# Attention and gated feed-forward in one kernel: fp32 weights by hardware DMA with casts on ACT and VectorE, and a first batch loaded in 1 KB rows

## The chip, the cores and the metric

The kernel runs on one core of one Trainium2 chip. The metric is the device time of one execution in microseconds (us). The chip's engines are called PE (TensorE), ACT (ScalarE), DVE (VectorE), POOL (GpSimd) and SP (SyncE). POOL and SP issue the DMAs here.

## The reference, cut to what matters

```python
# q, k, v: (8 batches, 8 heads, 576, 64) fp32; global_idx: 8 positions
scores = (q @ k^T) / 8, kept where |i - j| <= 32, or i or j is a global position
x = softmax(scores) @ v             # heads side by side: 4608 tokens x 512
g, val = x @ w_gate, x @ w_val      # 512 x 1536 each
ffn_out = (gelu(g) * val) @ w_out   # 1536 x 512
out = x + sigmoid(x @ w_res) * ffn_out   # 4608 x 512 fp32
```

All inputs are fp32. The kernel computes in bf16 with fp32 accumulation.

## The kernel before

The 4608 tokens are cut into nine *chunks* of 512. A *stage* is the feed-forward of one chunk: twelve blocks of up-projection (`ffn_in`, 8 matmuls each), then sixteen steps of down-projection (`ffn_out`). The attention of the next chunk is woven into the down-projection. Chunk c + 1 has tokens of batches c and c + 1, so the weave of stage c needs batch c + 1 to be loaded.

Everything that arrives as fp32 and is wanted as bf16 is loaded by POOL, whose DMA casts on the way. Only the first batch's Q and K come raw through SP. The parts that the change touches:

```python
def load_qk(b):                       # POOL, casting: 10 DMAs in 256 B rows
    for src, dst in ((q, q_st), (k, k_st)):
        for r in range(NQT):
            ...
            nc.gpsimd.dma_start(dst[0:n, r, :]..., src[b]...)

def load_v(b):                        # POOL, casting: 5 DMAs into ve[b % 2]
    ...
def shift_v(b):                       # SP: vo[b % 2] is ve moved by 64 partitions
    nc.sync.dma_start(vo[b % 2][0:64, ...], ve[b % 2][64:128, ...])
    nc.sync.dma_start(vo[b % 2][64:128, ...], ve[b % 2][0:64, ...])
def turn_qk(b):                       # SP: 10 DMA transposes, q_st -> qt, k_st -> kt
    ...
def zero_rest(i, eng):
    eng.memset(ve[i][:, :, :, D:VG], 1.0)      # V's column of ones: L161
    eng.memset(ve[i][0:32, 0, :, :], 0.0)
    ...                                        # five more small ones

# first batch: raw Q and K, a head pair at a time, on 96 partitions
for p in range(NP):
    for src, what in ((q, "q"), (k, "k")):
        nc.sync.dma_start(raw[what][0:QP, ...], src[0, 2 * p:2 * p + 2]...)
...
gather("k", 0); gather("q", 0); zero_rest(0, nc.gpsimd); load_v(0); gather("v", 0)
load_gate_cols(0, 512)
... # masks, transposes and scores of batch 0
load_gate_cols(512, 1024)
...
load_qk(1)
load_gate_cols(1024, 1536)
load_v(1)
nc.gpsimd.dma_start(wr_t, ...)
for h0 in range(0, NFF, 6):
    nc.gpsimd.dma_start(wo_t[:, h0:h0 + 6, :], ...)
for n in range(1, B // 2):            # nine gathers of the global rows
    for what in "kqv":
        gather(what, n)
...
for c in range(NCH):
    b = c + 1
    if b < B:
        if c == 0: zero_qk(1)
        turn_qk(b)
        if b > 1: load_v(b)
    for j in range(NFF):
        ffn_in(c, j)
        if b < B:
            if c == 0 and j == 1:
                zero_rest(1, nc.vector)        # after load_v(1) in program order
                hot_rows(1)
            ...
            if j == 8:
                shift_v(b)
                if b + 1 < B: load_qk(b + 1)
                prep_qz(b, 0, NP)
            if j == 11:
                held = global_scores(b)        # sg (needs qt), ss (needs kt)
    ... # scores, values, turn_x of chunk c + 1 woven into ffn_out(c)
```

`turn_x(c, t)` makes the transposed x of a chunk. For c > 0 the tiles 0 to 2 go through SP's DMA transpose and tile 3 through PE.

The softmax here doesn't subtract the row's maximum and nothing guards it: scores larger than these inputs give would overflow.

## Time and profile before

| | before |
|---|---|
| median of the runs | 433.5 us (432.92 to 435.04, 4 runs) |
| profiled span | 431.6 us |
| PE busy | 386.6 us, 90% of the span |
| mean granted PE clock | 0.974 |
| up-projection of chunk 0 | 34.3 to 77.5 us, 20.2 of it idle |
| first matmul of chunk 1's up-projection | 98.8 us |
| stage 1 | 42.9 us |

The two rows below are from the page's busy digits of the kernel before. Each digit is the busy share, in tenths, of one fortieth of the span (10.8 us).

```profile
PE   2578009999999999999999999999999999999995
DMA  7999998949997999399849992996296130021001
```

The zeros in the fifth and sixth place are the gap. The DMA row is full from the second to the sixth slice, so the gap falls where the DMA engines have no room. From the seventh slice on PE has no hole. The next view cuts the same stretch into pieces. Its columns are the window, its length, then the busy time and instruction count of PE, PEld, DVE, ACT and POOL, then the granted clock, a DMA share (not used here) and GB/s.

```profile
43.99:64.21 20.22, 0.00 (x1) 0.00 (x0) 1.92 (x7) 0.00 (x0) 8.04 (x10) 0.59 1.55 160
...
77.34:98.82 21.48, 21.32 (x210) 13.44 (x212) 11.11 (x23) 10.34 (x16) 10.59 (x12) 1.00 1.06 109
```

In the first row PE, PEld and ACT do nothing for 20.2 us while DMA goes on. In the last row, the down-projection of chunk 0 with the attention of chunk 1 in it, PE is busy for 21.3 of 21.5 us.

### The profile page before, as it was taken

How to read it: one execution, taken by the hardware profiler on the slowest of the kernel's cores; microseconds unless marked ns; L12 is line 12 of the kernel's file. 1: busy time of each engine (PE TensorE's matmuls, PEld its weight loads, DVE VectorE, ACT ScalarE, POOL GpSimd, SP SyncE). 2: the span in 40 equal slices, each digit the busy share in tenths (PEclk: the TensorE clock that was granted, in tenths of full speed). 3: DMA queues.
4: the chain of work that ended last, by engine and by line, in shares of the span. 5: the costliest groups of instructions: out<-in, count | busy, mean ns of one | idle time of the engine just before them, and what ended most of it. 6: DMA issues, size and time to landing. Idle time of an engine off the chain costs nothing.

```text
span 431.6 us, 7189 instructions
## 1 busy us (share of the span) xinstructions
PE 386.6 (90%) x2749; PEld 208.9 (48%) x2794; DVE 209.6 (49%) x396; ACT 169.6 (39%) x274; POOL 167.9 (39%) x194
## 2 busy tenths in 40 slices
PE   2578009999999999999999999999999999999995
PEld 1363004654465446544654565456545654564442
DVE  6774027554656355535544554356435644463421
ACT  5455002623462336333623462345235423533320
POOL 6577252915492471257125712561330120022012
PEclk9999758999999999999999999999999999999999
DMA  7999998949997999399849992996296130021001
GB/s 173 169 178 155 161 164 170 109 93 112 146 92 111 101 178 120 66 124 182 88 87 112 185 89 77 128 184 73 74 147 93 38 98 1 0 75 62 0 26 74
DMA packets 164642, 46.56 MB, mean 108 GB/s; under 512 B 152128, under 2 KB 158784, under 8 KB 164608
## 3 DMA queue, kind: packets, MB, share of 16 engines
q0 software_dynamic: 108784, 18.62, 60.5%
q1 hardware_dynamic: 55824, 27.48, 33.0%
q8 instruction: 22, 0.36, 0.4%
q14 instruction: 12, 0.10, 0.1%
HBM read 39.19 MB, written 9.44 MB: 113 GB/s over the span
## 4 chain that ended last, share of the span: by engine, by line
PE 74%; issue 8%; POOL 1%; DVE 1%; POOLq 0%; DVEq 0%
PE f_ps L432 19%; PE v_ps L409 18%; PE g_ps L405 17%; PE r_ps L422 6%; PE nd L373 4%; PE sc L347 3%; PE nd L367 2%; PE sn L335 2%; PE sg L313 2%; POOL ob L438 1%; PE ss L318 1%; DVE qz L306 1%; PE tx L397 0%; POOLq L570 0%; DVE ht L413 0%
## 5 line engine op out<-in xcount | busy, mean ns | idle before, releaser
L409 PE MATMUL v_ps<-xt,wv_t 128*128 128x512 bf16 x431 | 111.8, 382 | 21.0 <-DVE ht L413 20.4
L412 ACT ACTIVATE gsb<-g_ps 128x512 bf16<-128x512 f32 x108 | 64.5, 597 | 145.8 <-PE g_ps L405 112.4
L413 DVE SCALAR_TENSOR_TENSOR ht<-gsb,v_ps 128x512 bf16<-128x512 bf16 x108 | 73.9, 687 | 91.7 <-PE v_ps L409 90.1
L438 POOL TENSOR_TENSOR ob<-prb,xtok 128x512 f32<-128x512 f32 x36 | 41.9, 1164 | 193.3 <-DVE prb L436 193.2
L405 PE MATMUL g_ps<-xt,wg_t 128*128 128x512 bf16 x415 | 109.4, 381 | 1.1 <-ACT xt L398 0.7
L432 PE MATMUL f_ps<-wo_t,ht 128*128 128x512 bf16 x412 | 102.0, 380 | 1.0
L409 PEld LDWEIGHTS <-wv_t 128*128 128x128 bf16 x432 | 42.5, 98 | 72.5 <-issue 22.3
L405 PEld LDWEIGHTS <-wg_t 128*128 128x128 bf16 x432 | 42.4, 98 | 52.0 <-issue 1.9
L432 PEld LDWEIGHTS <-ht 128*128 128x128 bf16 x432 | 38.4, 98 | 34.0
L350 ACT ACTIVATE pt<-sc 128x512 bf16<-128x512 f32 x72 | 41.8, 597 | 29.1 <-PE sc L347 29.0
L425 ACT ACTIVATE rsb<-r_ps 128x512 bf16<-128x512 f32 x36 | 21.4, 596 | 62.0 <-PE r_ps L422 58.0
L352 DVE TENSOR_TENSOR pt<-pt,maskw 128x512 bf16<-128x512 bf16 x72 | 31.8, 444 | 26.7 <-ACT pt L350 25.6
L90 POOL DMA_DIRECT2D q_st<-in_q_dram x35 | 29.8, 868 | 24.0 <-DMA qt<-q_st 24.0
L436 DVE SCALAR_TENSOR_TENSOR prb<-rsb,f_ps 128x512 f32<-128x512 bf16 x36 | 24.6, 684 | 29.4 <-PE f_ps L432 29.2
L422 PE MATMUL r_ps<-wr_t,xt 128*128 128x512 bf16 x137 | 36.6, 379 | 0.4
L98 POOL DMA_DIRECT2D ve<-in_v_dram x40 | 34.3, 869 | 1.9 <-DMA k_st<-in_k_dram 1.9
L90 POOL DMA_DIRECT2D k_st<-in_k_dram x35 | 30.8, 908 | 2.8 <-issue 1.2
L347 PE MATMUL sc<-qz,kt 128*128 128x128 bf16 x288 | 27.8, 224 | 0.0
L347 PEld LDWEIGHTS <-kt 128*128 128x128 bf16 x288 | 21.7, 100 | 12.1
L387 DVE TENSOR_TENSOR xtok<-nd,rden 128x512 bf16<-128x512 f32 x34 | 23.5, 692 | 1.2
L373 PEld LDWEIGHTS <-pt 128*128 128x128 bf16 x576 | 22.3, 97 | 1.8 <-DMA vo<-ve 0.8
L373 PE MATMUL nd<-ve,pt 128*128 128x65 bf16 x320 | 22.4, 193 | 0.0
(104 smaller groups left out, 259.7 us busy)
## 6 DMA issues: line engine op xcount, KB each, us to landing
out_dram<-ob SPq DMA_DIRECT2D x36, 256.0 KB, 2.1
vo<-ve SPq DMA_DIRECT2D x16, 260.0 KB, 5.7
q_st<-in_q_dram POOLq DMA_DIRECT2D x28, 128.0 KB, 5.0
k_st<-in_k_dram POOLq DMA_DIRECT2D x28, 128.0 KB, 6.1
ve<-in_v_dram POOLq DMA_DIRECT2D x24, 128.0 KB, 6.7
ve<-in_v_dram POOLq DMA_DIRECT2D x16, 96.0 KB, 6.0
wg_t<-in_moe_w_gate_dram POOLq DMA_DIRECT2D x3, 512.0 KB, 5.9
wv_t<-in_moe_w_val_dram POOLq DMA_DIRECT2D x3, 512.0 KB, 12.7
```

Source lines behind the costliest of these rows:

```text
L90: nc.gpsimd.dma_start(dst[0:n, r, :].rearrange("p (h d) -> p h d", d=D), src[b].rearrange("h s d -> s h d")[128 * r:128 * r + n])
L98: nc.gpsimd.dma_start(t[p0:p1, c, :, 0:D], v[b].rearrange("h s d -> s h d")[s0 + p0:s0 + p1])
L347: nc.tensor.matmul(sc[:, n, :, :], kt[b % 2][:, p, 64 * i:64 * i + 128], qz[b % 2][:, p, :, 64 * i:64 * i + 64], start=True, stop=True)
L350: nc.scalar.activation(mine, sc, ACTF.Exp, bias=0.0, scale=SCALE)
L373: nc.tensor.matmul(nds[h // 4][:, VG * (h % 4):VG * (h % 4) + VG], view(pt, 0, 128, c0, [[1, 128]]), vw, start=False, stop=(h % 4 == 3 and ...
L405: nc.tensor.matmul(g_ps, wg_t[:, kk, 128 * j:128 * j + 128], x[:, kk, :], start=(kk == 0), stop=(kk == NKT - 1))
L409: nc.tensor.matmul(v_ps, wv_t[:, kk, 128 * j:128 * j + 128], x[:, kk, :], start=(kk == 0), stop=(kk == NKT - 1))
L412: nc.scalar.activation(gsb, g_ps, ACTF.Gelu, bias=0.0, scale=1.0)
L413: nc.vector.scalar_tensor_tensor(ht[:, j, :], gsb, 0.5, v_ps, ALU.mult, ALU.mult)
L422: nc.tensor.matmul(r_ps, xt[c % 2][:, kk, 128 * t:128 * t + 128], wr_t[:, kk, :], start=(kk == 0), stop=(kk == NKT - 1))
L432: nc.tensor.matmul(held["f"], ht[:, j, 128 * t:128 * t + 128], wo_t[:, j, :], start=(j == 0), stop=(j == NFF - 1))
L438: nc.gpsimd.tensor_tensor(ob, prb, xtok[c % 2][:, t, :], ALU.add)
```

## The change

The intent is to take the weights out of POOL's queue. Each weight is cut into fp32 pieces of 512 KB, loaded by SP's hardware DMA into tiles that are not needed until batch 1, and cast from there by DVE and ACT between the blocks of chunk 0. The first batch's raw Q and K come in 1 KB rows on all 128 partitions, and the scores run as each head pair arrives. Because the pieces occupy tiles of batch 1, that batch is loaded later than before.

```diff
+    slots = [flat32(qz[1], 0), flat32(qz[1], 1024), flat32(xt[1], 0), flat32(xtok[1], 0), flat32(vo_flat[1], 0),
+             flat32(kt[1], 0), flat32(qt[1], 0), flat32(ve_flat[1], 0)]
+    pieces = [...]          # 12 of w_gate and w_val, 2 of w_res, 6 of w_out
+    def load_piece(n):
+        nc.sync.dma_start(staged(n), pieces[n][0])
+    def cast_piece(n, copy):
+        copy(pieces[n][1], staged(n))
+        nxt = NSL + n if n < NRE else n + NRE if n >= NSL else len(pieces)
+        if nxt < len(pieces):
+            load_piece(nxt)
-    RPP = 6
+    RPP = 4
 ...
     for c in range(NCH):
         b = c + 1
         if b < B:
-            if c == 0:
-                zero_qk(1)
-            turn_qk(b)
-            if b > 1:
+            if c:
+                turn_qk(b)
                 load_v(b)
         for j in range(NFF):
             ffn_in(c, j)
             if b < B:
                 if c == 0:
+                    ... # cast_piece(4) to cast_piece(19), one or two a block
-                    if j == 1:
+                    if j == 6:
+                        zero(q_st[:, :, 0:1])
+                        zero(k_st[:, :, 0:1])
+                        load_qk(1)
+                    elif j == 9:
                         zero_rest(1, nc.vector)
+                        load_v(1)
                         hot_rows(1)
+                    elif j == 11:
+                        shift_v(1)
                 if c == 1:
+                    if j == 0:
+                        for n in range(1, B // 2):
+                            for what in "kqv":
+                                gather(what, n)
 ...
+        if c == 0:
+            jobs[0] += [lambda: zero_qk(1), lambda: turn_qk(1)]
+            jobs[4].append(ready)          # prep_qz(1, 0, NP); load_qk(2)
+            jobs[5].append(second)         # global_scores(1)
+            ...
+            for t in range(4):
+                jobs[(11, 12, 14, 15)[t]].append(lambda t=t: values(1, t))
+                jobs[(13, 14, 16, 16)[t]].append(lambda t=t: turn_x(1, t))
```

`jobs[n]` runs ahead of step n of the down-projection, and `jobs[16]` after the last step. Numbers of steps below are these.

## The prediction

> **What bounds the kernel now.** I read the page first: PE is busy 90% of the span, and from slice 8 on its digits are all 9, so the seven later stages are matmul time and nothing that the change does to them can give much. The room is in the first 80 us. There I read the timelines of PE, of VectorE (DVE), of GpSimd (POOL) and of the sync queue in turn. PE first (columns: start us, duration us, engine, line, operation, count, idle time before it):
>
> ```profile
> 42.97 1.03 PE L405 MATMUL g_ps<-xt,wg_t 128*128 128x512 bf16 x4
> 64.21 1.87 PE L409 MATMUL v_ps<-xt,wv_t 128*128 128x512 bf16 x4 [20.22 <-DVE ht L413]
> ...
> 77.34 1.14 PE L313 MATMUL sg<-qt,kgz 128*128 128x288 bf16 x8
> ```
>
> The up-projection of chunk 0 starts at 34.3, stops at 44.0 and resumes at 64.2. The first group after the gap takes 1.87 us where a warm one takes 1.03: a cold clock, worth some 2 us until 68.7. Without the gap, 12 column blocks at 2 x 0.864 us would take 20.7 us; they take 43. What held `ht` stands in DVE's timeline:
>
> ```profile
> 38.06 0.69 DVE L413 SCALAR_TENSOR_TENSOR ht<-gsb,v_ps 128x512 bf16<-128x512 bf16 x1 [1.05 <-PE v_ps L409]
> 61.88 0.09 DVE L161 MEMSET ve<- 128x40 bf16 x1 [23.14 <-DMA ve<-in_v_dram]
> ```
>
> The memset of V's ones column for batch 1 waits in program order for V of batch 1 to land, and that load sits in GpSimd's queue behind the weights. DVE stands still, and four to five blocks later so does PE. Behind that is a full DMA system: the DMA row of the page is at 9 until about 72 us. The gap is thus partly an order problem and partly a lack of DMA time. What batch 1 needs after its loads is in the sync queue, here for batch 2:
>
> ```profile
> 101.50 6.63 SPq L302 DMA_TRANSPOSE qt<-q_st  x5
> 108.24 6.45 SPq L302 DMA_TRANSPOSE kt<-k_st  x5
> ```
>
> Ten DMA transposes take 13.2 us of issue, and in the other stages it is 13.4 to 14.6. In GpSimd's timeline the loads that come before them take:
>
> ```profile
> 120.52 4.26 POOL L90 DMA_DIRECT2D q_st<-in_q_dram  x5
> 124.74 4.24 POOL L90 DMA_DIRECT2D k_st<-in_k_dram  x5
> ...
> 143.86 4.24 POOL L98 DMA_DIRECT2D ve<-in_v_dram  x5
> ```
>
> So Q, K and V of one batch are 8.5 + 4.2 us[...], and the page gives some 6 us (5.0 to 6.7) from issue to landing.
>
> [...]raw Q/K by hardware DMA, V by GpSimd and part of the first weights together fill the DMA row from 5 to 19 us.[...] Here the raw loads on 96 partitions ran at 240 to 250 GB/s, the 128-partition output stores at about 370.[...]
>
> **The change part by part.**
>
> (1) *Raw loads.* 2.36 MB at 245 GB/s were 9.6 us. At an estimated 330 GB/s (between 245 and 370[...]) they are 7.2 us, plus a little for the tails in 256 B rows. DVE, though, bounds this part, and it now also does the six mask products of pairs 0 to 2 (6 x 0.44 = 2.6 us) before the global keys are spread. It also meets the doubling of the gathered rows in the third pair, at about 15.5 us; the gather of q now follows V in GpSimd's queue (issued at about 12) and should land near 17.5. I put the spread at 22 us against 18.9 before. Afterwards six products fewer lie in the way, so the up-projection starts at about 34.5 against 34.3. A wash, within 1.5 us.
>
> (2) *Weights.* 10.5 MB fp32 at 330 GB/s are 32 us of DMA against 25.6 us before (5.24 MB written at 205 GB/s). The first piece can go when V of batch 0 has landed and been shifted, at about 17.5 us. At 1.6 us each, pieces 0 to 3 are in by 26, 4 to 11 by 39. They are needed at 34.5 and, two at a time, every 3.5 us from 41. Casts: ACT 0.83 us for 768 columns, so about 1.1 for 1024; DVE 0.56, so about 0.7. In a block of 1.73 us ACT has 0.6 + 1.1 and DVE 0.69 + 0.7: they fit. Weights should not stop PE in the up-projection. It loses its gap and ends at 34.5 + 20.7 = 55.
>
> (3) *Batch 1 is moved behind the weights.* This is what I expect to decide. Its Q and K loads are issued after block 6, its V after block 9, the shift of V after block 11, and its transposes only behind that shift in the same sync queue. Working it out from the rows above:
> - block 6 evicted, piece 10 cast, the small memset: 34.5 + 7 x 1.73 + 0.3 + 0.7 + 0.9 = 48.5;
> - Q/K issue 8.5, V issue 4.2: 61.5;
> - last V landed, 6: 67.5 (later if the last six weight pieces, some 9 us of DMA, delay it);
> - two shifts issued, 1.1: 68.5;
> - ten transposes 13, landing of the last 3: 84.5.
>
> Five of the 16 down-projection steps are placed ahead of global_scores(1): 5 x 0.86 = 4.3, so PE is out of work at about 59.5. PE then waits in order for qt and kt until about 84.5: some 25 us in place of the 20 us that were removed. The query half can run when qt has landed.
>
> (4) *Rest of chunk 0.* Before, from sg(1) at 77.5 to the next up-projection at 98.8 is 21.3 us. Without the five steps (4.3) and sg (1.0) 16 us remain: 84.5 + 16 + 2 for the cold clock = 102.5.
>
> (5) *A new tail.* The transposes of x for tiles 2 and 3 of chunk 1 now come after the last step. Tile 2's is a DMA transpose behind the last output store in the sync queue. Before, that store was issued at 101.4 where the last f_ps ended at 99.0, that is 2.4 later; with 2.4 of median landing for the transpose PE waits 4.8 us, and may cool again (1). Next up-projection: 102.5 + 5.8 = 108.3, against 98.8: +9.5 us.
>
> (6) *Gathers in stage 1.* Nine at 1.25 us of GpSimd time behind V of batch 2; the doubling that needs them stands at about 15 us in that stage. They should arrive at 15 to 17.5; before, DVE stood from 38.8 and PE only from 43.9, a slack of 5 us. Cost nothing, at most 2.
>
> Sum: 433.8 + 9.5 = 443.3, say **443 us**.
>
> **The rivals.**
> *The gap simply goes* (faster, about 415): the memset no longer waits for V, the weights arrive early, PE runs through. For it speaks that the 20 us gap is the only large one and its cause is really removed. Against it, the chain of (3): even with 4.5 us of landing, 12 us of transposes and a start at 33, qt and kt are there only at 79.5, and five steps of work do not cover 24 us.
> *A draw* (428 to 438): loads are quicker than I think, the DMA system having less to do by then, and the tail is shorter. The best sum above gives 79.5 + 16 + 1 + 4.5 = 101, +2 us. So a draw needs most terms at their good end.
> *The weights become the bound* (450 or more): if 1 KB rows run at 200 GB/s, the twelve gate and value pieces are in only at about 51, the casts then hold DVE and ACT in order, zero_rest(1) and with it V of batch 1 go later, and every term of (3) moves. Against it, 2 KB rows at 370 GB/s and 1.5 KB at 245[...].
>
> **Range and chances.** The start of the up-projection is uncertain by 1.5 us, the landing of V by 4 (mostly upward), the transposes by 2, the tail by 3, the rates of weights by 3; together about 7 either way, with a longer arm upward: 434 to 453. 2% is 8.7 us, so the border to slower lies at 442.5, just below my middle: slower 0.52, same 0.43. Faster would need the chain of (3) to be wrong by 18 us: 0.05.
>
> **What would show it.** Right: no wait of DVE on in_v_dram at L161's memset; PE through the up-projection of chunk 0 in about 21 us; then one idle stretch of some 20 us before global_scores(1), released by DMA into qt or kt; the sync queue with the V shift ahead of ten transposes issued between about 68 and 82; an idle stretch of about 5 us before chunk 1's first gate matmul, released by the DMA into xt; stages 2 to 7 unchanged within 0.5 us each. Wrong: PE working through the down-projection of chunk 0, which would mean that transposes ended by about 60; or gaps inside the up-projection before wg_t or wv_t, which would mean that the weights bind; or a first stage several us from 34.5.

The 330 GB/s for the new loads are the author's estimate, between the 245 GB/s of the raw loads and the 370 GB/s of the output stores in the kernel before. "Cold clock" stands for what that trace shows: the granted clock is 0.50 from 64.2 to 68.0 us and 1.00 from 68.7, and the three groups of matmuls from 64.21 to 68.71 take 4.5 us where warm ones take 2.6. That is the 2 us in (4). The 1 us in (5) is a guess from it. A short wait was followed by the same in the kernel after: 3.8 us idle until 59.59, then a granted clock of 0.60 until 63.86.

## The result and the profile after

A ratio is the mean time of one kernel's runs over that of the other's runs in the same rounds, so it is not quite the ratio of the medians quoted.

| | before | after |
|---|---|---|
| median | 433.5 us | 455.44 us (454.59 to 455.94, 4 runs) |
| ratio | 1 | 1.0498 (95%: 1.0466 to 1.053) |
| profiled span | 431.6 us | 453.2 us |
| mean granted PE clock | 0.974 | 0.947 |
| up-projection of chunk 0 | 34.3 to 77.5 | 34.0 to 54.9 |
| global_scores(1) ends | 79.0 | 89.35 |
| chunk 0's last down-projection matmul ends | 99.0 | 108.2 |
| chunk 1's up-projection starts | 98.8 | 117.0 |
| stage 1 | 42.9 | 46.2 |
| all that follows | 289.9 | 290.0 |

The kernel is 5.0% slower. All of the 21.6 us between the spans lies ahead of stage 2: 18.15 us where chunk 1 starts and 3.3 us in stage 1. These are the digits of the kernel after, with slices of 11.3 us.

```profile
PE   3579940395689999999999999999999999999995
DMA  7997999934992259939983994499289130013001
```

The hole of before has moved by a slice or so, to the sixth to eighth place (4, 0 and 3), and there is a second dent at the tenth and eleventh. The DMA row is at 9 through PE's hole and falls only after it, to 3 and 4 in the ninth and tenth place. A full row beside an idle PE does not tell whether too much was asked of the DMA engines or whether it was asked in the wrong order; the experiments have to. The windows of the kernel after, with the same columns as before:

```profile
34.02:54.91 20.89, 20.89 (x97) 9.50 (x97) 12.65 (x26) 14.00 (x19) 6.58 (x8) 1.00 0.93 246
...
63.90:89.35 25.45, 4.45 (x34) 2.26 (x33) 3.38 (x6) 1.88 (x2) 10.35 (x12) 0.56 1.54 141
...
108.17:116.97 8.80, 0.40 (x5) 0.26 (x6) 1.12 (x3) 0.00 (x0) 7.33 (x8) 0.68 1.07 99
```

The first row is the success of the change: PE is busy for all of the 20.9 us of the up-projection. The other two rows are its price, 21 and 8.4 us of idle PE. What ended them is in PE's timeline of the kernel after (start, duration, engine, line, operation, count, idle time before it and its releaser):

```profile
59.59 4.44 PE L472 MATMUL f_ps<-wo_t,ht 128*128 128x512 bf16 x12 [3.82 <-ACT gsb L452]
...
77.71 1.12 PE L353 MATMUL sg<-qt,kgz 128*128 128x288 bf16 x4 [12.82 <-DMA qt<-q_st]
...
89.07 0.28 PE L358 MATMUL ss<-qgz,kt 128*128 128x16 bf16 x4 [0.71 <-DMA kt<-k_st]
...
116.97 1.86 PE L445 MATMUL g_ps<-xt,wg_t 128*128 128x512 bf16 x4 [8.24 <-DMA xt<-xtok]
118.63 1.91 PE L449 MATMUL v_ps<-xt,wv_t 128*128 128x512 bf16 x4
120.33 1.68 PE L445 MATMUL g_ps<-xt,wg_t 128*128 128x512 bf16 x4
```

The first line is a wait outside the rows above: PE stands 3.8 us between the up-projection and the down-projection, because ACT waits for a piece of w_out to arrive before its cast. It costs nothing here, since PE runs out of work at 64.9 us anyway. Then comes the wait for the transposed queries, next that for the transposed keys, last that for the transposed x of chunk 1. The three groups after the last wait take 1.68 to 1.91 us at a granted clock of 0.52 (116.97 to 121.85 us) where a warm one, at 1.00, takes 1.03. Why `qt` came so late is in SP's and POOL's timelines of the kernel after. SP:

```profile
70.30 0.47 SPq L104 DMA_DIRECT2D vo<-ve  x1
...
71.46 7.49 SPq L342 DMA_TRANSPOSE qt<-q_st  x5
79.05 6.48 SPq L342 DMA_TRANSPOSE kt<-k_st  x5
...
110.65 1.25 SPq L433 DMA_TRANSPOSE xt<-xtok  x1
```

POOL:

```profile
48.34 4.78 POOL L92 DMA_DIRECT2D q_st<-in_q_dram  x5 [20.69 <-PE v_ps L449]
53.11 4.33 POOL L92 DMA_DIRECT2D k_st<-in_k_dram  x5
57.53 0.78 POOL L100 DMA_DIRECT2D ve<-in_v_dram  x1
61.88 3.41 POOL L100 DMA_DIRECT2D ve<-in_v_dram  x4 [3.56 <-DMA q_st<-in_q_dram]
```

Read from POOL upwards: Q and K are issued at 48 to 57 us, V follows and stands for 3.56 us in the middle, the shift of V waits in SP until 70.3, and only behind it, in the same queue, come the ten transposes. The queries needed nothing from V. They stood behind it.

### The profile page after: what moved, and what is told of

Read it like the earlier page. It is cut to its first block, busy times and chain, and to the rows that moved or that the text cites. A ratio compares the mean times of both kernels' runs of the same rounds, so it can differ in the third digit from the quotient of the medians. Undisturbed runs are those within 1.5% of the kernel's fastest.

```text
span 453.2 us, 7270 instructions
## 1 busy us (share of the span) xinstructions
PE 397.2 (88%) x2786; PEld 211.2 (47%) x2786; DVE 214.9 (47%) x408; ACT 180.3 (40%) x288; POOL 160.1 (35%) x185
## 3 DMA queue, kind: packets, MB, share of 16 engines
q0 software_dynamic: 103520, 13.38, 51.5%
q1 hardware_dynamic: 65904, 37.96, 36.5%
## 4 chain that ended last, share of the span: by engine, by line
PE 75%; DMA 8%; issue 6%; POOL 4%; SPq 3%; DVE 2%; ACT 1%; POOLq 0%; DVEq 0%
PE g_ps L445 20%; PE v_ps L449 20%; PE f_ps L472 17%; PE r_ps L462 6%; PE nd L413 3%; PE sc L387 3%; SPq L342 2%; DMA q_st<-in_q_dram 2%; PE sg L353 2%; PE nd L407 2%; POOL ve L100 2%; DMA qgf<-in_q_dram,idx 2%; PE sn L375 1%; DMA ve<-in_v_dram 1%; DMA xt<-xtok 1%
## 5 line engine op out<-in xcount | busy, mean ns | idle before, releaser
L453 DVE SCALAR_TENSOR_TENSOR ht<-gsb,v_ps 128x512 bf16<-128x512 bf16 x108 | 74.2, 688 | 110.8 <-PE v_ps L449 103.1
L445 PE MATMUL g_ps<-xt,wg_t 128*128 128x512 bf16 x432 | 112.3, 383 | 9.1 <-DMA xt<-xtok 8.2
L472 PE MATMUL f_ps<-wo_t,ht 128*128 128x512 bf16 x432 | 109.7, 390 | 3.8 <-ACT gsb L452 3.8
L472 PEld LDWEIGHTS <-ht 128*128 128x128 bf16 x432 | 39.4, 100 | 40.1 <-issue 7.7
L92 POOL DMA_DIRECT2D q_st<-in_q_dram x35 | 30.3, 881 | 56.8 <-DMA qt<-q_st 34.5
L392 DVE TENSOR_TENSOR pt<-pt,maskw 128x512 bf16<-128x512 bf16 x72 | 34.1, 480 | 26.4 <-ACT pt L390 25.0
L465 ACT ACTIVATE rsb<-r_ps 128x512 bf16<-128x512 f32 x36 | 21.5, 596 | 58.8 <-PE r_ps L462 47.5
L387 PE MATMUL sc<-qz,kt 128*128 128x128 bf16 x288 | 29.1, 230 | 0.8 <-DVE qz L346 0.7
L387 PEld LDWEIGHTS <-kt 128*128 128x128 bf16 x288 | 22.7, 104 | 14.4 <-DVE qz L346 1.3
L353 PE MATMUL sg<-qt,kgz 128*128 128x288 bf16 x64 | 11.2, 325 | 19.1 <-DMA qt<-q_st 16.5
L346 DVE COPY qz<-qt 64x2304 bf16<-64x2304 bf16 (+1 forms) x22 | 14.8, 671 | 17.6 <-DMA qt<-q_st 16.9
```

The costliest lines, as they stand in the source:

```text
L92: nc.gpsimd.dma_start(dst[0:n, r, :].rearrange("p (h d) -> p h d", d=D), src[b].rearrange("h s d -> s h d")[128 * r:128 * r + n])
L387: nc.tensor.matmul(sc[:, n, :, :], kt[b % 2][:, p, 64 * i:64 * i + 128], qz[b % 2][:, p, :, 64 * i:64 * i + 64], start=True, stop=True)
L392: nc.vector.tensor_tensor(mine, mine, view(maskw, 0, 128, 64 * i0, [[64, 4], [0, 2], [1, 64]]), ALU.mult)
L445: nc.tensor.matmul(g_ps, wg_t[:, kk, 128 * j:128 * j + 128], x[:, kk, :], start=(kk == 0), stop=(kk == NKT - 1))
L453: nc.vector.scalar_tensor_tensor(ht[:, j, :], gsb, 0.5, v_ps, ALU.mult, ALU.mult)
L472: nc.tensor.matmul(held["f"], ht[:, j, 128 * t:128 * t + 128], wo_t[:, j, :], start=(j == 0), stop=(j == NFF - 1))
```

## The experiments

Twelve kernels ran, each timed in three rounds against the kernel before. All agreed with the reference, e3_no_wo too (see there). "ss ends" is the end of global_scores(1). "C1 starts" is the first up-projection matmul of chunk 1. Both are from the PE timeline of the profiled run.

| run | made from | median us | ratio (95%) | ss ends | C1 starts | stage 1 |
|---|---|---|---|---|---|---|
| before | | 433.5 | 1 | 79.0 | 98.8 | 42.9 |
| after | | 455.44 | 1.050 (1.047 to 1.053) | 89.35 | 117.0 | 46.2 |
| e1_tail | after | 450.63 | 1.038 (1.033 to 1.043) | 90.7 | 110.8 | 48.2 |
| e2_turn_first | after | 445.14 | 1.027 (1.024 to 1.031) | 79.5 | 106.1 | 46.7 |
| e3_no_wo | after | 450.2 | 1.038 (1.034 to 1.041) | 84.5 | 112.5 | 46.3 |
| e4_order | before | 426.82 | 0.985 (0.982 to 0.988) | 61.8 | 91.75 | 42.9 |
| e5_tail_gathers | after | 444.0 | 1.025 (1.022 to 1.029) | 89.3 | 109.3 | 42.4 |
| e6_late_qk2 | after | 455.77 | 1.052 (1.047 to 1.057) | 87.4 | 118.8 | 44.7 |
| e7_early | after | 435.35 | 1.006 (1.003 to 1.009) | 75.2 | 99.2 | 44.5 |
| e8_order_v | before | 426.85 | 0.986 (0.984 to 0.989) | 66.7 | 90.8 | 42.9 |
| e9_early_pe | after | 430.23 | 0.992 (0.989 to 0.995) | 76.6 | 96.7 | 42.6 |
| e10_raw_order | before | 427.82 | 0.988 (0.984 to 0.993) | 68.5 | 93.7 | 42.9 |
| e11_raw_only | before | 434.91 | 1.003 (1.000 to 1.006) | 83.3 | 103.2 | 42.9 |
| e12_hybrid | after | 429.08 | 0.991 (0.987 to 0.995) | 71.9 | 93.7 | 42.9 |

The theory after the result had four parts: the order V, shift, transposes in SP's queue sets the end of global_scores(1); the last weight pieces delay V; the new DMA transpose at the end of chunk 0 costs its landing; the gathers cost something in stage 1. The rival is that the DMA engines are simply full, in which case a new order moves nothing. The first four runs take these one at a time.

### e1_tail: the last tile of x for chunk 1 turned by PE instead of by DMA

```diff
-        if c and t < 3:
+        if c and t < 3 and not (c == 1 and t == 2):
```

> The changed kernel with one edit: tile 2 of chunk 1 is turned on TensorE like tile 3, not by a DMA transpose behind the last output store. Theory (the new tail costs what the trace shows): the idle stretch of 8.2 us before chunk 1's first gate matmul shrinks to about 1 us and TensorE stays warm, which saves another 2.3 us; about 445.5 us, at least 443 and at most 449. Rival (the stretch is only slack in front of the next wait, for instance the batch 2 loads or the gathers in stage 1): stage 1 gives it back and the time stays at 453 to 456.

Measured: 450.63 us. The time from the last down-projection matmul to chunk 1 falls from 8.8 to 1.5 us (109.32 to 110.83), so 7.3 us of it were the DMA transpose, and the groups behind it are warm, 1.02 to 1.03 us each. The total misses the range of the theory (443 to 449) and that of the rival too. It falls by only 4.8 us, because stage 1 grew from 46.2 to 48.2 us and because the profiled chain happened to end 1.35 us later. The growth in stage 1 is a new standstill. This is ACT's timeline of this run:

```profile
120.53 0.60 ACT L452 ACTIVATE gsb<-g_ps 128x512 bf16<-128x512 f32 x1 [1.13 <-PE g_ps L445]
126.25 0.60 ACT L452 ACTIVATE gsb<-g_ps 128x512 bf16<-128x512 f32 x1 [5.13 <-issue]
```

ACT's input was there at about 122.2 us (the g_ps group that starts at 121.19 takes 1.03), and ACT took it at 126.25. "issue" means that the trace shows nothing that it waited for. DVE stood in the same time, and PE stopped behind them. The nine gathers were being issued from 115.8 to 126.9 us.

### e2_turn_first: the transposes ahead of the shift of V in SP's queue

```diff
                     elif j == 11:
+                        turn_qk(1)
                         shift_v(1)
 ...
-            jobs[0] += [lambda: zero_qk(1), lambda: turn_qk(1)]
+            jobs[0] += [lambda: zero_qk(1)]
```

> The changed kernel with one edit: in the sync queue the ten transposes of batch 1 stand ahead of the V shift. Theory (the serial chain Q/K loads, V load, shift, transposes sets when chunk 0's down-projection goes on): the transposes start some 10 us earlier, at about 61, end at about 75 and land by 79; the wait before and in global_scores(1) loses about 10 us; 445 us, 443 to 448. Rival (DMA capacity decides, order does not): transposes and V share the same engines, so the last landing moves by at most 3 us and the time stays above 452.

Measured: 445.14 us, as the theory had it. Global scores end 9.8 us earlier, with the same transfers (the page of the kernel after counts both queues on the same 16 engines: 51.5% of their span for POOL's, 36.5% for SP's). The order in the queue is thus worth 10 us of the loss, and the rival of plainly full DMA engines falls as the main cause. PE's waits in this run (engine, line, releaser; us in total, times, longest):

```profile
PE sg L353 <- DMA qt<-q_st: 6.0, 2, 4.6
PE ss L358 <- DVE kt L188: 4.4, 1, 4.4
```

The wait for `qt` fell from 16.5 to 6.0 us. The next one is made by the edit itself: the memset of `kt`'s borders now comes after the transposes into `kt` in program order, and waits for them.

### e3_no_wo: the last six weight pieces (w_out) not loaded, their casts left in; a wrong result

```diff
-        if nxt < len(pieces):
+        if nxt < 14:
```

> The changed kernel with the six loads of moe_w_out left out (3.1 MB less to load between 45 and 61 us; the casts read what lies in the places, so the result is wrong on purpose). Theory (serial issue and order decide): only the 3.6 us that GpSimd stood before the second V load go, and a little of the landing; 450 to 452. Rival (DMA capacity decides): all of the 9 us that these pieces take goes: 445 to 447.

Measured: 450.2 us, 5.2 less than the kernel after and within the theory's range; the rival (445 to 447) is refuted. Global scores end at 84.5 us, where the prediction had put them without a delay by these pieces. That it is exactly there is luck: the last V landed at 65.55 us, 2.0 earlier than predicted, and the transposes and their landing took 1.8 us longer. POOL's timeline of this run shows the V loads in one run, without the 3.56 us, and SP's shows the shift 4.7 us earlier:

```profile
57.09 4.33 POOL L100 DMA_DIRECT2D ve<-in_v_dram  x5
```

```profile
65.62 0.47 SPq L104 DMA_DIRECT2D vo<-ve  x1
...
66.77 7.51 SPq L342 DMA_TRANSPOSE qt<-q_st  x5
```

So the six pieces (3.1 MB) in the DMA engines beside Q, K and V are what delayed V. The semaphore records in the two traces show by what path. The fourth Q load landed 10.5 us after its issue in the kernel after, and 4.2 us after it here. In its record, the V load that stood waits for the semaphore of this Q load, issued eight loads before it: POOL's loads use eight semaphores in turn (110 to 117 in the trace of the kernel after). The kernel before shows the same: each of the twelve longer waits of POOL's issues for a DMA from 33 to 75 us (0.5 to 4.8 us) is for the one issued eight before. So the 3.56 us of standing are a wait of the program for a slow transfer. The last V load was issued 3.9 us later and took 6.4 us to land in place of 4.9; together V was complete at 70.90 us in place of 65.55. The result still passed the comparison with the reference: at the size of the drawn inputs its tolerance does not see these weights. Passing it therefore says nothing for w_out, in this kernel or in any other here, but the other kernels load all of it.

### e4_order: the kernel before, with zero_rest(1) at the very start on POOL

```diff
+    zero_rest(1, nc.gpsimd)
     gather("k", 0)
 ...
                     if j == 1:
-                        zero_rest(1, nc.vector)
                         hot_rows(1)
```

> The kernel before with one edit: the constants of batch 1's V tile are set by GpSimd at the very start instead of by VectorE behind the V load. It takes away the wait that made the 20 us gap and nothing else. Theory (the gap is half an order problem): TensorE runs on to the down-projection of chunk 0 and then waits for moe_w_out, which still lands at about 72: 8 to 10 us saved, 424 to 427. Rival (the gap was DMA time and only moves): 431 to 434.

Measured: 426.82 us, 1.5% faster than the kernel before and by far the best of the first four. One call, moved to the start and from DVE to POOL, takes DVE's wait for V away with no other part of the change. The up-projection ends at 60.4 us instead of 77.5. But chunk 1 starts only 7.1 us earlier, not 17, and PE's waits in this run say why:

```profile
PE f_ps L433 <- DMA wo_t<-in_moe_w_out_dram: 5.1, 2, 4.4
PE v_ps L410 <- DMA wv_t<-in_moe_w_val_dram: 1.9, 1, 1.9
PE g_ps L406 <- DMA wg_t<-in_moe_w_gate_dram: 1.5, 1, 1.5
PE r_ps L423 <- DMA wr_t<-in_moe_w_res_dram: 1.4, 1, 1.4
```

The gap of 20 us was worth some 7 us. The rest of it had been covering weights that were not there yet.

### e5_tail_gathers: e1_tail, and the nine gathers at step 4 of chunk 0 instead of in stage 1

```diff
-                    if j == 0:
-                        for n in range(1, B // 2):
-                            for what in "kqv":
-                                gather(what, n)
-                    elif j == 7:
+                    if j == 7:
 ...
             def ready():
                 prep_qz(1, 0, NP)
+                for n in range(1, B // 2):
+                    for what in "kqv":
+                        gather(what, n)
                 load_qk(2)
```

> The changed kernel with the tail edit of e1 and one more: the nine gathers go into GpSimd's queue ahead of the Q/K loads of batch 2, where GpSimd stood idle, not into stage 1. Theory (e1 gave only half of its 10 us because ScalarE and TensorE stand some 4 us in stage 1 while the gathers, V loads and transposes fill the DMA queues): that standstill shrinks to under 1 us, 446 to 447. Rival (the standstill comes from the V loads and transposes alone, the gathers move nothing): 450 to 451 as e1.

Measured: 444.0 us, 6.6 less than e1_tail and 2 us better than the theory's range; the rival is refuted. Stage 1 takes 42.4 us, against 48.2 there. The standstill goes when the gathers are moved, but their place alone does not make it. In e6_late_qk2 (next) they are issued in stage 1 as well, from 116.1 to 127.2 us, beside the V loads and transposes of the next batch, and ACT keeps its pace. POOL and ACT there:

```profile
126.23 0.94 POOL L230 DMA_INDIRECT vgf<-in_v_dram,idx  x1 [0.30 <-issue]
...
125.69 0.60 ACT L452 ACTIVATE gsb<-g_ps 128x512 bf16<-128x512 f32 x1 [1.13 <-PE g_ps L445]
```

What else differs is in the traces. Those in which ACT and DVE stand in stage 1 (the kernel after, e1, e2 and e3) lack most landing records of the DMAs of just these microseconds; of the nine gathers of e1_tail, eight have none or one of 16. The traces of e5, e6 and the kernel before lack none. So the recording itself may have a part in the standstill. This is not shown either way: every timed run here was recorded. By what path the gathers stop ACT and DVE, and whether they would without the recording, stays open.

### e6_late_qk2: the Q and K loads of batch 2 from step 4 to step 12

```diff
             def ready():
                 prep_qz(1, 0, NP)
-                load_qk(2)
 ...
+            jobs[12].append(lambda: load_qk(2))
```

> The changed kernel with one edit: the Q/K loads of batch 2 go into GpSimd's queue eight steps later, so they do not share the DMA engines with batch 1's last transposes. Theory (the last key transposes landed 5 us after issue and not 3 because of them): global_scores(1) ends some 2 to 3 us sooner, 452 to 453.5. Rival (landing is the transposes' own): no gain, 455 to 456.

Measured: 455.77 us, no gain. This was a miss for the theory as a time, and its mechanism half held: the five transposes of K now landed 2.4 to 2.5 us after their issue, against 3.5 to 5.0 in the kernel after, and global scores ended 1.9 us earlier. But the moved loads fell on the end of the chunk. PE's waits, POOL and SP in this run:

```profile
PE g_ps L445 <- DMA xt<-xtok: 11.7, 1, 11.7
```

```profile
110.47 1.17 POOL L478 TENSOR_TENSOR ob<-prb,xtok 128x512 f32<-128x512 f32 x1
...
112.10 1.24 SPq L433 DMA_TRANSPOSE xt<-xtok  x1
```

The wait for `xt` was 8.2 us before the edit. The path is again the order of queues. POOL issues these loads until 110.45 us, its last addition for the output comes behind them, SP's store waits for that, and the transpose stands behind the store. It is issued 5.6 us after the last matmul, 2.5 before the edit; its landing took 6.5 us, hardly more than the 6.2 before. A load taken off one wait came to lie ahead of another.

### e7_early: Q and K of batch 1 from block 0, V from block 4, the shift last, with the edits of e5_tail_gathers

```diff
-                    if j == 6:
+                    if j == 0:
                         zero(q_st[:, :, 0:1])
                         zero(k_st[:, :, 0:1])
                         load_qk(1)
-                    elif j == 9:
+                    elif j == 4:
+                        zero_kt(1)
                         zero_rest(1, nc.vector)
                         load_v(1)
 ...
+                    for n in {6: (0,), 7: (1,), 8: (2,), 9: (3,), 10: (4, 5), 11: (6, 7)}.get(j, ()):
+                        turn_one(1, n)            # one DMA transpose each
 ...
-            jobs[0] += [lambda: zero_qk(1), lambda: turn_qk(1)]
+            jobs[0] += [lambda: zero_qz(1), lambda: turn_one(1, 8), lambda: turn_one(1, 9), lambda: shift_v(1)]
```

> The changed kernel with the weights as it has them, but with batch 1 early: Q/K loads after block 0, V after block 4, the transposes one by one between blocks 6 and 11, the V shift last; plus the edits of e5. Theory (the order of batch 1's chain, not the way the weights come, costs the time): the wait before global_scores(1) shrinks from 25 us to under 8; 424 to 432, below the kernel before. Rival (DMA capacity decides: 32 us of weights plus 14 us of Q, K and V cannot be in by 60 us): the wait moves into the up-projection before wg_t or wv_t or before wo_t, and the time stays at 437 or more.

The 32 us are the prediction's estimate, 10.5 MB at 330 GB/s. The 14 us fit an estimate too: 3.54 MB of Q, K and V at the 245 GB/s of the raw loads in the kernel before.

Measured: 435.35 us, between what the two expected. The wait before global scores is down to 2.3 us for `kt`. Two others took its place, as PE's waits show:

```profile
PE g_ps L459 <- DMA xt<-xtok: 4.6, 1, 4.6
PE f_ps L486 <- ACT wo_t L135: 4.6, 2, 2.4
PE f_ps L486 <- DVE wo_t L135: 2.5, 2, 1.3
```

The casts of w_out now come late; Q, K, V and the transposes went first. And the tail is back: the gathers and the Q and K loads of batch 2 keep POOL in its own queue until 92.5 us, its additions for the output come after them, the stores wait for those, and the transposes of x stand behind the stores in SP.

### e8_order_v: e4_order, with V of batch 1 behind the weights of the down-projection

```diff
-    load_v(1)
     nc.gpsimd.dma_start(wr_t, ...)
     for h0 in range(0, NFF, 6):
         nc.gpsimd.dma_start(wo_t[:, h0:h0 + 6, :], ...)
+    load_v(1)
```

> The kernel before with the edit of e4 and V of batch 1 loaded behind moe_w_res and moe_w_out in GpSimd's queue. Theory (in e4 TensorE waits 5 us for moe_w_out, and V is not needed before the shift): moe_w_out lands some 5 us sooner, 421 to 424. Rival (DMA capacity: V late stops global_rows(1) and the values instead): 426 to 429.

Measured: 426.85 us, the same as e4_order; the rival was right. The wait for `wo_t` is gone and one for the transposed keys has come, since more of the weights now go beside the ten transposes in the DMA engines. This is the wait in PE's view and the five transposes of K in SP's timeline, which took 11.8 us in e4_order and 6.5 in the kernel after:

```profile
PE ss L319 <- DMA kt<-k_st: 3.4, 2, 2.7
```

```profile
42.19 14.84 SPq L303 DMA_TRANSPOSE kt<-k_st  x5
```

This points to the DMA engines as the bound here: a new order changes what PE waits for, and hardly the time.

### e9_early_pe: e7_early, with the gathers directly behind V and all of chunk 1's x turned by PE

```diff
                         load_v(1)
+                        for n in range(1, B // 2):
+                            for what in "kqv":
+                                gather(what, n)
 ...
-        if c and t < 3:
+        if c > 1 and t < 3:
```

> As e7, with two edits: the gathers follow V of batch 1 in GpSimd's queue, so the Q/K loads of batch 2 no longer hold back the residual additions and with them the output stores; and all of chunk 1's turns of x are made on TensorE. Theory (e7 lost 4.6 us before chunk 1's first gate matmul and 2.5 us to a cold clock behind it, both through the sync queue): 428 to 430. Rival (the tail's wait only covers the lack of DMA time): 433 to 436.

The cold clock meant here is in e7_early's PE timeline: the three groups behind the wait of 4.6 us take 4.8 us, from 99.23 to 104.02, where three warm ones take 2.6.

Measured: 430.23 us, 0.2 above the range of the theory (428 to 430) and far from the rival's. The tail is 1.5 us and stage 1 is 42.6 us. The largest waits left are PE's for w_out's casts: 3.9 us for ACT's and 2.1 for DVE's.

### e10_raw_order and e11_raw_only: the first batch's part of the change, alone

The edit is the first part of the change's diff (rows of 1 KB on 128 partitions, scores pair by pair), put on the kernel before (e11_raw_only) and on e8_order_v (e10_raw_order).

```diff
-    RPP = 6
+    RPP = 4
 ...
+    for p in range(-1, NP):
+        load_raw(k, "k", p)
+        load_raw(q, "q", p)
```

> The kernel before with the order of e8, plus the first part of the change alone (first batch in 1 KB rows on all partitions, scores pair by pair). Theory (the raw loads are done some 2 to 3 us sooner and everything behind them in the full DMA queues moves up by that): 422 to 424.5. Rival (the part is a wash, as I predicted for it): 426 to 428.

> The kernel before with the first part of the change alone, the rest of its order as it was. Theory of the prediction (a wash for the start of the up-projection): 432.5 to 434.5. Rival (sooner raw loads free DMA time, V of batch 1 lands sooner and the 20 us gap ends sooner): 429 to 431.5.

Measured: 427.82 us for e10_raw_order and 434.91 for e11_raw_only, both within half a per cent of their bases. Chunk 0's up-projection starts at 34.3 and 34.1 us, where it did before. This part neither gains nor loses. Both theories that had the sooner loads gain something (422 to 424.5 for e10, 429 to 431.5 for e11) are refuted. In the profiled run of e11_raw_only, the slowest of its five (438.03 us), the old gap is even longer: the last V load of POOL's queue is issued at 48.1 us and not at 43.6. PE's wait is 20.4 us in the kernel before:

```profile
PE v_ps L419 <- DVE ht L423: 24.1, 2, 23.9
```

### e12_hybrid: e9_early_pe, with w_res and w_out by POOL's casting DMA again

```diff
                         load_qk(1)
+                        nc.gpsimd.dma_start(wr_t, ...)
+                        for h0 in range(0, NFF, 6):
+                            nc.gpsimd.dma_start(wo_t[:, h0:h0 + 6, :], ...)
```

Only the twelve pieces of w_gate and w_val are then staged and cast.

> As e9, but only the gate and value weights come as fp32 by the sync queue; moe_w_res and moe_w_out are again cast by GpSimd's DMA, issued after batch 1's Q/K. Theory (in e7 TensorE waits 7 us for casts of moe_w_out that stand in line behind loads and places): 422 to 427. Rival (DMA capacity): the same waits turn into waits for the DMA into wo_t, 428 to 431 as e9.

Measured: 429.08 us, above the 422 to 427 expected. The waits for casts turned into waits for the transfers themselves:

```profile
PE f_ps L482 <- DMA wo_t<-in_moe_w_out_dram: 5.8, 2, 3.5
PE r_ps L472 <- DMA wr_t<-in_moe_w_res_dram: 2.2, 1, 2.2
```

This is the rival of a full DMA system, and here it holds. The best kernels are e4_order and e8_order_v at 426.8 us. Both beat the kernel before and the kernel after, and neither contains any of the change.

## Why the prediction was wrong in size and right in kind

The direction, the place and the mechanism were right. The time was 455.4 us where 443 was given and 453 was the upper end. Two terms were mis-sized: the landing of V in step 3, and in step 5 the transpose of x with the cold clock behind it. I go through the prediction's own steps.

1. **Raw loads: right.** The up-projection started at 34.0 us (34.5 predicted), and e11_raw_only gives 1.003 for this part alone. The loads did get faster: in e11_raw_only a raw load of K lands 5.1 us after its issue and one of Q 4.8 (medians of four), where the kernel before has 7.0 and 6.2 for pieces an eighth larger, and the core moves some 250 to 370 GB/s in those microseconds where it moved about 250. The estimate of 330 GB/s was fair. Whether the longer rows or the 128 partitions made the loads faster is not shown; the two were not changed apart.

2. **Weights: right.** The up-projection ran without a gap to 54.9 us (55 predicted). A cast of 1024 columns took 1.04 us on ACT and 0.69 us on DVE (1.1 and 0.7 predicted). The memset of the ones column waited for nothing: DVE's timeline of the kernel after has it at 52.94 us.

```profile
52.94 0.09 DVE L200 MEMSET ve<- 128x40 bf16 x1
```

3. **Batch 1 behind the weights: mechanism right, one term mis-sized.** Issue of Q and K began at 48.3 us (48.5 predicted). The chain was as described, but its end was 89.35 us and not 84.5. The failed term is "last V landed, 6: 67.5 (later if the last six weight pieces, some 9 us of DMA, delay it)". The prediction named the delay and priced it at zero in its sum. V landed at 70.9 us, 3.4 late; the rest of the 4.85 us is transposes of 14.1 us for 13 and a last landing of 3.8 for 3, less 0.5 for the shifts. Without those six pieces V landed at 65.55 and global scores ended at 84.5 (e3_no_wo), so the pieces cost 4.85 us, and that the two 4.85 are equal is the luck told there. (A slip in the sum: 48.5 + 8.5 + 4.2 is 61.2 and not 61.5.) That the order in SP's queue decides was shown by e2_turn_first, which takes 10.3 us off the total.

4. **Rest of chunk 0: right.** 18.8 us against the 18 predicted.

5. **The tail: place right, size wrong.** The transpose was issued 2.5 us after the last matmul (2.4 predicted), but PE went on only 6.3 us after that issue, where the step took 2.4 "of median landing". At that moment POOL issued the five V loads of batch 2 (from 110.1 us), and the median of 24 landings in the kernel before did not fit. The tail was 8.8 us, and 4.8 were given for it, 5.8 with the cooling. e1_tail shows that it is the DMA transpose. That loads beside it lengthen it is supported by the records of landing: the two earlier transposes of chunk 1's x in the same run, ahead of the V loads, landed 4.2 and 2.9 us after their issue, the last one 6.2; in e6_late_qk2, with loads beside all three, they took 6.5 to 6.8. The V loads alone were not taken away.

6. **Gathers: within the bound, for another reason; the cold clock: wrong in size.** Stage 1 grew by 3.3 us. Some 2.3 us are the three cold groups after the tail (they took 4.9 us from 116.97 to 121.85 where three warm ones take 2.6); step 5 had 1 us for this. A wait of PE for `ht` in the time of the gathers took 1.4 us, within "cost nothing, at most 2". But the prediction looked for the cost at the doubling that needs the gathers, and not for a standstill of ACT and DVE. In e1_tail, with the tail removed and the clock warm, that came out larger: 48.2 us for the stage against 42.4 in e5_tail_gathers, with the doubt about the recording told there.

The sum: 9.5 us predicted, and 4.85 (step 3) + 0.8 (step 4) + 3.0 (step 5) + 3.3 (step 6) on top are 21.5, against 21.6 between the spans. All that follows stage 1 moved by 0.1 us, as predicted. The three experiments that each remove one of these terms agree: e5_tail_gathers without the tail and the gathers is at 444.0, and if e3_no_wo's 5.2 us are taken off that as well, 438.8 remain. That last figure is an estimate from two runs and was not run itself.

Of the rivals, the one in which the gap simply goes was refuted by the windows. Its underlying value can now be given: removing that gap is worth 6.6 us (433.4 to 426.8 in e4_order) and not 20. The rival of a draw was wrong for this order, but it describes the repaired kernels: e9_early_pe at 430.2 and e12_hybrid at 429.1. The rival in which the weights bind did not occur in the up-projection. Behind it PE waited 3.8 us for a cast of w_out in the kernel after, hidden by the longer wait that followed; when batch 1 goes first, such waits show (e7_early and e9_early_pe).

What stays open: how the gathers stop ACT and DVE and whether the recording has a part in it, and what the V loads alone add to the transpose of the tail.

## What to carry to other kernels

A gap that ends when a DMA lands has two prices: what waits behind it in program order, and what would not be there yet anyway (here 20.2 us of gap, and 6.6 us of gain in e4_order). Try the one-line reorder first (here one call that holds six small memsets, moved to the start, gave 1.5%), because it shows how much of the gap is order. When transfers are moved to make room, follow the displaced ones through the order of every queue to the next consumer (9.8 us to the end of global scores from the order in SP's queue alone, e2_turn_first), and price each landing with what will be in flight beside it then, not with a median (6.2 us against 2.4 for the transpose of the tail). A DMA transpose on the last step before a dependent matmul should go to the PE if PE would only wait for it (e1_tail: 8.8 us fell to 1.5).
